# Scaling the attention scores by 0.125 as they leave PSUM, with the negated row maximum written by VectorE

## The chip, the core and the metric

The program runs on one core of a Trainium2 chip. The core has five engines with in-order queues: TensorE (PE, with its weight loads as PEld), VectorE (DVE), ScalarE (ACT), GpSimd (POOL) and SyncE (SP, which here only starts DMA transfers). An engine takes the next instruction of its own queue only when that one's semaphores allow it, so an instruction that waits holds up everything queued behind it on its engine. The metric is the device time of one execution in microseconds; lower is better.

## What is computed

Three blocks run one after the other. The change touches the first, attention that keeps the 32 largest scores of every row:

```python
scores = scale * np.matmul(q, k.transpose(0, 1, 3, 2))      # scale = 1/sqrt(64) = 0.125
kth    = np.partition(scores, -32, axis=-1)[..., -32:-31]
scores = np.where(scores >= kth, scores, -1e9)
attn   = np.exp(scores - scores.max(-1)); attn /= attn.sum(-1) + 1e-9
out    = attn @ v                                            # 4 batches, 8 heads, 576 x 576, head size 64
```

The other two ("dense" below) are a token-mixing block with a squared ReLU and a sigmoid gate, and a block with GELU, a layer norm and a 576 x 576 matrix over the tokens. All of it is float32; matmuls are made of three passes over operands split into a high and a low part.

## The kernel before

**Tiles.** The rows of the score matrices are cut into 80 slots of 128 rows: per batch 4 head pairs, each with five slots, of which four hold the same 128 rows of two heads (n = 2) and one the last 64 rows of both (n = 1). Batch 0 goes through its slots in two halves.

**One slot.** `emit_S` makes the scores on PE into the PSUM tile `S`, and ACT copies them to SBUF (`S2`, line 242, or line 255 for the slot with n = 1). `emit_topk` searches on DVE: lines 275 and 276 take the elementwise larger and smaller of the two row halves into `T`; four rounds of `max` (line 284, the next eight of a row) and `match_replace` (line 294, strikes them out) lead to the 32nd value. After the second round's `max` a small reduce (line 287) has the row maximum, ACT multiplies it by -0.125 (line 288, tile `nb`), and ACT's exponential (line 306) computes `E = exp(0.125 * S + nb)`, two instructions for n = 2. `emit_mask` (line 311, DVE) zeroes what lies below the 32nd value and sums the rest; it is emitted in the next slot, between that slot's first `match_replace` and its second round. Then `emit_T` transposes E on PE (line 326 and its neighbours) with copies to SBUF on ACT (line 327, `PT`), and after the last slot of a unit `emit_unit` multiplies by v (line 355, for the last batch line 386), copies the row factors with ACT (line 413, `rb`) and writes the result with DVE (line 420, `x`).

**Dense work** of a batch (`part1`, `part2`) becomes available when the attention of the batch is complete, and is mixed into the slots of the next batch; the dense work of the last batch is left for the end. Lines 569, 634, 679, 760 and 788 are its matmuls, 686 and 534 its copies and GELUs on ACT, 695 to 700 its layer norm on DVE and POOL, 518 its weight loads on SP. The split into high and low parts is ACT line 100 and POOL line 102.

**What sets the order.** Each piece of work gets a priority (`at(1000 * s)` for slot s), and a list scheduler lays out the engines' queues by priority and by when it reckons an instruction's inputs to be ready. So one instruction more or less shifts the order of many others. The exponential needs another set of tables on ACT than the GELU; a table load stands in the queue at each switch.

Line 275 to 311 are what the change touches; the quoted functions follow.

Of the kernel before, what the change touches and what calls it, by code (L numbers as in the profile page):

```python
# [9 lines left out]
F32 = mybir.dt.float32  # L10
# [3 lines left out]
AF = mybir.ActivationFunctionType  # L14
OP = mybir.AluOpType
# [8 lines left out]
def computation(ctx, tc, dram, wscr, flag, fast, q, k, v, mu_k, mu_r, w_k, w_v, w_r, w_in, g_ln, w_sg, b_sg, w_out, out):  # L24
    nc = tc.nc
# [8 lines left out]
    HALF = S // 2  # L34

    const = ctx.enter_context(tc.tile_pool(name="const", bufs=1))
    sb = ctx.enter_context(tc.tile_pool(name="sb", bufs=1))
# [46 lines left out]
    def bank(tag, shape=(128, 512), dt=F32):  # L84
        if tag == "d" and rows[0] == NROWS:
            tag = ("d", "tp")[turn[0] % 2]
            turn[0] += 1
        return psum.tile(list(shape), dt, tag=tag, name=tag, bufs=BUFS[tag])
# [22 lines left out]
    for b in range(B):  # L111
# [4 lines left out]
        for p, chs in order:  # L116
            su = Rec()
            su.b, su.p, su.chs, su.raw, su.slots = b, p, chs, {}, []
            for ch in chs:
# [3 lines left out]
                for i, j in enumerate(js):  # L123
                    t = Rec()
# [107 lines left out]
    def emit_S(t):  # L232
        su = t.su
        t.S = sb.tile([128, t.hs, S], F32, tag="S2", name="S2", bufs=3)
        for h in range(t.hs):
            ps = bank("S", (128, 2, 512))
            if t.j < 4:
                for a in range(2):
                    for hf in range(2):
                        nc.tensor.matmul(ps[:, hf, :HALF], lhsT=su.qst[h, t.u.ch][:, a, 128 * t.i:128 * t.i + 128],  # L240
                                         rhs=su.kst[h][:, HALF * hf:HALF * hf + HALF], start=(a == 0), stop=(a == 1))
                nc.scalar.activation(t.S[:, h].rearrange("p (a n) -> p a n", a=2), ps[:, :, :HALF], AF.Copy)  # L242
            else:

                for i in range(4):
                    hh, a = divmod(i, 2)
                    ks, qs = su.kst[hh], su.qrem[:, a, hh:hh + 2].rearrange("p h m -> p (h m)")
                    if hh == 0:
                        parts = [(0, 0, 0, HALF), (1, 0, HALF, HALF)]
                    else:  # L250
                        parts = [(0, 0, 64, HALF), (1, 0, 64 + HALF, 512 - HALF), (1, 512 - HALF, 0, 64)]
                    for hf, o, ko, m in parts:
                        nc.tensor.matmul(ps[:, hf, o:o + m], lhsT=qs, rhs=ks[:, ko:ko + m],
                                         start=(i == 0), stop=(i == 3 and m != 512 - HALF))
                nc.scalar.activation(t.S[:, 0].rearrange("p (a n) -> p a n", a=2), ps[:, :, :HALF], AF.Copy)

    ROUNDS = (slice(0, 208), slice(48, HALF), slice(0, HALF), slice(0, S))

    def emit_topk(t, between):

        u, n = t.u, t.hs
        if t.first:
            u.sums = sb.tile([128, 5], F32, tag="sums", name="sums", bufs=3)

            u.M = sb.tile([128, 5, 32], F32, tag="M", name="M", bufs=3)
            u.row0 = rows[0]
        c = 2 * t.i
        M = u.M[:, c:c + n]
        T = sb.tile([128, n, S], F32, tag="T2", name="T2", bufs=1)
        nb = sb.tile([128, n], F32, tag="nb", name="nb", bufs=3)  # L270
        t.E = sb.tile([128, n, S], F32, tag="E2", name="E2", bufs=2)
        if fast:

            for h in ([slice(h, h + 1) for h in range(n)] if rows[0] == 0 else [slice(0, n)]):
                nc.vector.tensor_tensor(T[:, h, :HALF], t.S[:, h, :HALF], t.S[:, h, HALF:], op=OP.max)  # L275
            nc.vector.tensor_tensor(T[:, :, HALF:], t.S[:, :, :HALF], t.S[:, :, HALF:], op=OP.min)  # L276
            L = [T[:, h, :] for h in range(n)]
            src, segs = L, ROUNDS
        else:
            L = [T[:, h, :] for h in range(n)]  # L280
            src, segs = [t.S[:, h, :] for h in range(n)], [slice(0, S)] * 4
        for r, seg in enumerate(segs):
            for h in range(n):
                nc.vector.max(M[:, h, 8 * r:8 * r + 8], src[h][:, seg])  # L284
            if fast and r == 1:
                top = sb.tile([128, n], F32, tag="top", name="top", bufs=3)
                nc.vector.tensor_reduce(top, M[:, :, 0:16:8], axis=mybir.AxisListType.X, op=OP.max)
                nc.scalar.activation(nb, top, AF.Copy, scale=-0.125)
            elif not fast and r == 0:
                nc.scalar.activation(nb, M[:, :, 0], AF.Copy, scale=-0.125)  # L290
            if r == 3:
                break
            for h in range(n):
                mr = nc.vector.match_replace(L[h][:, seg], M[:, h, 8 * r:8 * r + 8], src[h][:, seg], NEG)  # L294
            src = L
            if r == 0:
                between(mr)
        t.kv = [M[:, h, 31:32] for h in range(n)]
        if fast and t.last:

            m = c + n
            nc.gpsimd.tensor_tensor(gap[:, u.row0:u.row0 + m], u.M[:, :m, 31:32].to_broadcast([128, m, 3]),
                                    u.M[:, :m, 7:24:8], op=OP.subtract)
        rows[0] += n
        for h in range(n):
            nc.scalar.activation(t.E[:, h], t.S[:, h], AF.Exp, bias=nb[:, h:h + 1], scale=0.125)  # L306

    def emit_mask(t, gate):
        for h in range(t.hs):
# [545 lines left out]
    for i in range(AHEAD):  # L855
        emit_S(slots[i])
# [16 lines left out]
    for s, t in enumerate(slots):  # L873
# [4 lines left out]
        n = supers.index(su)  # L878
# [9 lines left out]
        if s + AHEAD < NS:  # L888
            emit_S(slots[s + AHEAD])
        emit_topk(t, lambda g: finish_slot(slots[s - 1], g) if s else None)  # L890
        if s == NS - 1:
            finish_slot(t, None)
# [21 lines left out]
    if fast:  # L914
        with at(1000 * NS):
            g = const.tile([128, 1], F32, name="g")
            nc.vector.tensor_reduce(g, gap.rearrange("p r i -> p (r i)"), axis=mybir.AxisListType.X, op=OP.max)
            ps = bank("tp")
# [69 lines left out]
```

## Time and profile before

| | us |
|---|---|
| median of 3 runs | 1001.49 |
| lowest and highest of them | 997.75, 1002.79 |
| the profiled execution's own time | 997.91 |
| its span, first to last instruction | 995.8 |
| DVE busy in the span | 841.0 (84%) |
| PE busy in the span | 878.1 (88%) |
| ACT busy in the span | 697.6 (70%) |
| POOL busy in the span | 528.7 (53%) |

Busy shares are averages over stages with different limits, so the views below are cut into stretches: attention with the conversion of the weights and the first dense work (25 to 660 us), the last batch's attention beside the dense work of the one before (660 to 803), a passage in which the attention ends (803 to 853), and the last batch's dense work (853 to 996). "Idle before" is time in which an engine stood still before an instruction, with what ended it. Records of matmuls overlap, so a PE that is busy all the time need not be at its peak.

### The profile page before, as it was taken

How to read it: one execution, taken by the hardware profiler on the slowest of the kernel's cores; microseconds unless marked ns; L12 is line 12 of the kernel's file. 1: busy time of each engine (PE TensorE's matmuls, PEld its weight loads, DVE VectorE, ACT ScalarE, POOL GpSimd, SP SyncE). 2: the span in 40 equal slices, each digit the busy share in tenths (PEclk: the TensorE clock that was granted, in tenths of full speed). 3: DMA queues.
4: the chain of work that ended last, by engine and by line, in shares of the span. 5: the costliest groups of instructions: out<-in, count | busy, mean ns of one | idle time of the engine just before them, and what ended most of it. 6: DMA issues, size and time to landing. Idle time of an engine off the chain costs nothing.

```text
span 995.8 us, 18647 instructions
## 1 busy us (share of the span) xinstructions
PE 878.1 (88%) x6078; PEld 759.7 (76%) x6078; DVE 841.0 (84%) x2337; ACT 697.6 (70%) x1559; POOL 528.7 (53%) x630
## 2 busy tenths in 40 slices
PE   3465768889888989798999999989999998999997
PEld 2344547777778888577888979868999886899895
DVE  6899999998999999999999999999999973712142
ACT  6778878888886796677687679666876585554340
POOL 7788788675975168559343216598331125210051
PEclk9986779999999999988999999999999999999999
DMA  7953486888467645512333343354333436664432
GB/s 214 371 187 136 156 252 224 282 279 304 167 209 252 219 120 188 171 33 69 109 100 110 110 143 94 99 192 151 109 118 109 128 124 223 218 248 148 122 126 68
DMA packets 105067, 166.34 MB, mean 167 GB/s; under 512 B 19328, under 2 KB 74368, under 8 KB 104960
## 3 DMA queue, kind: packets, MB, share of 16 engines
q1 hardware_dynamic: 104960, 165.05, 50.8%
q8 instruction: 50, 0.82, 0.3%
q14 instruction: 57, 0.47, 0.1%
HBM read 134.27 MB, written 30.21 MB: 165 GB/s over the span
## 4 chain that ended last, share of the span: by engine, by line
PE 45%; DVE 28%; ACT 10%; DMA 8%; POOL 4%; issue 3%; SPq 2%; POOLq 0%; DVEq 0%; ACTq 0%
PE d L569 9%; DVE M L284 8%; PE d L634 6%; DVE E L311 6%; DVE T L294 6%; PE d L679 5%; PE S L240 3%; PE d L760 3%; DVE T L275 3%; PE d L788 3%; PE tp L569 3%; DVE T L276 2%; PE tp L326 2%; PE tp L355 2%; ACT E L306 2%
## 5 line engine op out<-in xcount | busy, mean ns | idle before, releaser
L284 DVE MAX8 M<-T 128x8 f32<-128x208 f32 (+3 forms) x576 | 261.2, 485 | 1.0
L294 DVE MATCH_REPLACE8 T<-M,T 128x208 f32<-128x208 f32 (+2 forms) x432 | 168.9, 394 | 0.0
L569 PE MATMUL d<-xm,w 128*128 128x288 f32 (+2 forms) x1008 | 161.0, 305 | 6.9 <-DMA w<-ws_k 2.4
L311 DVE SCALAR_TENSOR_TENSOR E<-S,M,E 128x576 f32<-128x576 f32 x144 | 147.2, 1048 | 4.7 <-ACT E L306 4.7
L569 PEld LDWEIGHTS d<-xm,w 128*128 128x128 f32 x1008 | 140.5, 191 | 12.5 <-DMA w<-ws_k 3.2
L240 PE MATMUL S<-kst,qst 128*128 128x288 f32 x512 | 111.1, 337 | 28.6 <-ACT S L242 13.6
L240 PEld LDWEIGHTS S<-kst,qst 128*128 128x128 f32 x512 | 83.5, 209 | 41.5 <-ACT S L242 18.9
L326 PE MATMUL tp<-ident,E 128*128 128x128 f32 x512 | 84.6, 295 | 29.2 <-ACT kst L209 14.3
L306 ACT ACTIVATE E<-S,nb 128x576 f32<-128x576 f32 x144 | 105.2, 775 | 0.8
L634 PE MATMUL d<-ksq,w 128*128 128x288 f32 (+2 forms) x672 | 103.9, 302 | 0.6 <-DMA w<-ws_v 0.6
L242 ACT ACTIVATE S<-S 128x576 f32<-128x576 f32 x128 | 83.1, 650 | 30.2 <-DVE E L311 17.4
L326 PEld LDWEIGHTS tp<-ident,E 128*128 128x128 f32 x512 | 64.5, 150 | 38.2 <-ACT kst L209 15.0
L634 PEld LDWEIGHTS d<-ksq,w 128*128 128x128 f32 x672 | 91.8, 189 | 1.6 <-DMA w<-ws_v 0.8
L275 DVE TENSOR_TENSOR T<-S 128x576 f32<-128x576 f32 (+1 forms) x81 | 72.2, 891 | 17.3 <-ACT S L242 12.7
L327 ACT ACTIVATE PT<-tp 128x512 f32<-128x512 f32 x128 | 74.0, 599 | 8.5 <-PE tp L326 8.5
L276 DVE TENSOR_TENSOR T<-S 128x576 f32<-128x576 f32 (+1 forms) x80 | 79.8, 997 | 0.0
L355 PE MATMUL tp<-PT,rawv 128*64 128x256 f32 (+1 forms) x384 | 62.7, 461 | 9.1 <-ACT PT L327 9.1
L760 PE MATMUL d<-w,vn 128*128 128x288 f32 x392 | 60.1, 302 | 5.6 <-DMA w<-ws_sg 2.1
L697 POOL TENSOR_SCALAR bag<-bag 128x1 f32<-128x1 f32 (+1 forms) x20 | 6.1, 303 | 109.5 <-DVE bag L696 108.2
L102 POOL TENSOR_TENSOR ksq<-tmp,ksq 128x576 fp32r<-128x576 f32 (+2 forms) x32 | 41.1, 1289 | 37.3 <-ACT ksq L100 35.4
L760 PEld LDWEIGHTS d<-w,vn 128*128 128x128 f32 x392 | 53.7, 188 | 8.3 <-DMA w<-ws_sg 2.4
L788 PE MATMUL d<-w,gt 128*128 128x512 f32 (+1 forms) x204 | 53.8, 409 | 2.8 <-DVE xr L796 2.5
(182 smaller groups left out, 2018.3 us busy)
## 6 DMA issues: line engine op xcount, KB each, us to landing
w<-ws_k SPq DMA_DIRECT2D x40, 512.0 KB, 3.7
w<-ws_v SPq DMA_DIRECT2D x40, 512.0 KB, 4.1
w<-ws_sg SPq DMA_DIRECT2D x40, 288.0 KB, 3.7
w<-ws_r SPq DMA_DIRECT2D x20, 512.0 KB, 6.2
w<-ws_h SPq DMA_DIRECT2D x20, 512.0 KB, 3.6
w<-ws_u SPq DMA_DIRECT2D x20, 512.0 KB, 3.5
w<-ws_o SPq DMA_DIRECT2D x16, 512.0 KB, 4.6
rawk<-in_k_dram SPq DMA_DIRECT2D x40, 128.0 KB, 2.6
```

Of the source, the lines that this page charges most:

```text
L240: nc.tensor.matmul(ps[:, hf, :HALF], lhsT=su.qst[h, t.u.ch][:, a, 128 * t.i:128 * t.i + 128], rhs=su.kst[h][:, HALF * hf:HALF * hf + HALF] ...
L275: nc.vector.tensor_tensor(T[:, h, :HALF], t.S[:, h, :HALF], t.S[:, h, HALF:], op=OP.max)
L276: nc.vector.tensor_tensor(T[:, :, HALF:], t.S[:, :, :HALF], t.S[:, :, HALF:], op=OP.min)
L284: nc.vector.max(M[:, h, 8 * r:8 * r + 8], src[h][:, seg])
L294: mr = nc.vector.match_replace(L[h][:, seg], M[:, h, 8 * r:8 * r + 8], src[h][:, seg], NEG)
L306: nc.scalar.activation(t.E[:, h], t.S[:, h], AF.Exp, bias=nb[:, h:h + 1], scale=0.125)
L311: m = nc.vector.scalar_tensor_tensor(E, t.S[:, h], t.kv[h], E, op0=OP.is_ge, op1=OP.mult, accum_out=t.u.sums[:, 2 * t.i + h:2 * t.i + h + 1])
L326: nc.tensor.transpose(ps[:, kc, :], E[:, h, 64 * h + 128 * kc:64 * h + 128 * kc + 128], ident)
L569: nc.tensor.matmul(ps[:, :n_], lhsT=w[:, bb, 128 * c:128 * c + 128], rhs=act[ch, which, c][:, a, o:o + n_], start=(c == 0 and i == 0), sto ...
L634: nc.tensor.matmul(ps[:, :nn], lhsT=w[:, bb, 128 * (f % 4):128 * (f % 4) + 128], rhs=kt[f][:, a, o:o + nn], start=(f == 0 and i == 0), sto ...
L760: nc.tensor.matmul(ps[:, :HALF], lhsT=act[b, "vn", i][:, a, 128 * m:128 * m + 128], rhs=W["sg", i, si][:, bb, :HALF], start=(j == 0), stop ...
L788: nc.tensor.matmul(ps[:nn], lhsT=gt[m][:, a, 128 * i:128 * i + nn], rhs=W["o", m][:, bb, :512], start=(j == 0), stop=(j == 11))
```

## The change

The factor 0.125 moves from the exponential to the copy that takes the scores out of PSUM, so S, the search and the row maximum are in scaled units. The reduce on DVE writes the maximum negated, straight into `nb`; the tile `top` and the 80 small ACT instructions of line 288 are gone, and the exponential waits for DVE instead of for ACT's own earlier instruction. 0.125 is a power of two, so no score's digits change. (The kernel also holds a second version of the whole computation for inputs on which the short search is not exact; it is edited alike and is not executed here.)

```diff
-                nc.scalar.activation(t.S[:, h].rearrange("p (a n) -> p a n", a=2), ps[:, :, :HALF], AF.Copy)
+                nc.scalar.activation(t.S[:, h].rearrange("p (a n) -> p a n", a=2), ps[:, :, :HALF], AF.Copy,
+                                     scale=0.125)
...
-                top = sb.tile([128, n], F32, tag="top", name="top", bufs=3)
-                nc.vector.tensor_reduce(top, M[:, :, 0:16:8], axis=mybir.AxisListType.X, op=OP.max)
-                nc.scalar.activation(nb, top, AF.Copy, scale=-0.125)
+                nc.vector.tensor_reduce(nb, M[:, :, 0:16:8], axis=mybir.AxisListType.X, op=OP.max, negate=True)
...
-            nc.scalar.activation(t.E[:, h], t.S[:, h], AF.Exp, bias=nb[:, h:h + 1], scale=0.125)
+            nc.scalar.activation(t.E[:, h], t.S[:, h], AF.Exp, bias=nb[:, h:h + 1])
```

The queues of all engines are laid out anew. Three places matter below. The names are tiles, with their buffer's number where it is shown; 128x576 is the size of what is written.

ACT's queue around a slot in the second third of the program, before. L606 and L609 are dense copies, `ksq` the split that follows them, `rb` the row factors for the last product with v:

```order
L100 ACTIVATE ksq<-tmp 128x576
L242 ACTIVATE S_6490<-S 128x576
L606 ACTIVATE tmp<-d 128x288
L609 ACTIVATE tmp<-tmp 128x576
L100 ACTIVATE ksq<-tmp 128x576
L288 ACTIVATE nb<-top 128x2
L306 ACTIVATE E_6683<-S_6348,nb 128x576 x2
L413 ACTIVATE rb<-tp 128x320
L202 ACTIVATE qst<-tp 128x512
```

The same slot now (the line numbers are those of the changed file):

```order
L609 ACTIVATE tmp<-tmp 128x576
L100 ACTIVATE ksq<-tmp 128x576
L606 ACTIVATE tmp<-d 128x288
L242 ACTIVATE S_6400<-S 128x576
L306 ACTIVATE E_6591<-S_6260,nb 128x576 x2
L413 ACTIVATE rb<-tp 128x320
L202 ACTIVATE qst<-tp 128x512
```

The exponential stands where the copy of the maximum stood, with `rb` directly behind it as before; the pair of dense instructions that went ahead of it has changed.

PE's queue where the last slot's E is transposed (L334 to L339) and multiplied by v (L386 to L397) amid the token matrix (L760, 112 matmuls in two halves of 56), before:

```order
L334 MATMUL tp<-ident,E_11383 128x128 x4
L760 MATMUL d<-w,vn 128x288 x3
L338 MATMUL tp<-ident,E_11383 64x64
L339 MATMUL tp<-ident,E_11383 64x64
L760 MATMUL d<-w,vn 128x288 x6
L381 MATMUL tp<-identr,rhl 10x128
L386 MATMUL tp<-PT,rawv 64x320 x8
L390 MATMUL tp<-PTr,rawv 64x320 x2
L760 MATMUL d<-w,vn 128x288 x5
L392 MATMUL tp<-rT,spread 128x128 x2
L397 MATMUL tp<-rT,spreadr 128x64 x2
L760 MATMUL d<-w,vn 128x288 x65
```

And now:

```order
L334 MATMUL tp<-ident,E_11225 128x128 x4
L760 MATMUL d<-w,vn 128x288 x6
L338 MATMUL tp<-ident,E_11225 64x64
L339 MATMUL tp<-ident,E_11225 64x64
L381 MATMUL tp<-identr,rhl 10x128
L760 MATMUL d<-w,vn 128x288 x14
L386 MATMUL tp<-PT,rawv 64x320 x8
L390 MATMUL tp<-PTr,rawv 64x320 x2
L392 MATMUL tp<-rT,spread 128x128 x2
L397 MATMUL tp<-rT,spreadr 128x64 x2
L760 MATMUL d<-w,vn 128x288 x50
```

The first half of the token matrix is now through before the product with v; before, nine of its 56 matmuls came after that.

ACT's queue a little earlier, where the GELUs of the batch before last (L534) meet the exponential of the third slot from the end, before:

```order
L686 ACTIVATE vraw<-d 128x512
L534 ACT_TABLE_LOAD
L534 ACTIVATE vraw<-vraw 128x512
L686 ACTIVATE vraw<-d 128x512
L534 ACTIVATE vraw<-vraw 128x512
L686 ACTIVATE vraw<-d 128x512
L242 ACTIVATE S_11105<-S 128x576
L534 ACTIVATE vraw<-vraw 128x512
L327 ACTIVATE PT<-tp 128x4x128
L330 ACTIVATE PTr<-tp 128x128
L306 ACT_TABLE_LOAD
L306 ACTIVATE E_11218<-S_10965,nb 128x576 x2
```

And now:

```order
L686 ACTIVATE vraw<-d 128x512
L306 ACT_TABLE_LOAD
L306 ACTIVATE E_11064<-S_10815,nb 128x576 x2
L534 ACT_TABLE_LOAD
L534 ACTIVATE vraw<-vraw 128x512
L686 ACTIVATE vraw<-d 128x512
L242 ACTIVATE S_10953<-S 128x576
L534 ACTIVATE vraw<-vraw 128x512
L686 ACTIVATE vraw<-d 64x512
L534 ACTIVATE vraw<-vraw 128x512
L534 ACTIVATE vraw<-vraw 64x512
L242 ACTIVATE S_10953<-S 128x576
```

The exponential has moved ahead of the next slot's score copies (`S_11105` before, `S_10953` now), and the second of these now stands last, behind all the GELUs. The number of table loads in the program is unchanged.

## Rows read from the trace of the kernel before

**Rows 1.** Busy time by stretch: length, then PE, PEld, DVE, ACT, POOL, with counts.

```profile
core 0: us, PE busy (x) PEld busy (x) DVE busy (x) ACT busy (x) POOL busy (x), PEclk, DMA share, GB/s
25.00:660.00 635.00, 547.00 (x3829) 465.14 (x3829) 615.93 (x1734) 490.84 (x1117) 402.41 (x457) 0.94 0.54 176
660.00:803.00 143.00, 140.54 (x1001) 123.04 (x1000) 134.83 (x403) 98.39 (x223) 58.08 (x62) 0.99 0.38 122
803.00:853.00 50.00, 45.14 (x319) 38.54 (x318) 25.02 (x71) 31.50 (x60) 23.61 (x37) 1.00 0.58 189
853.00:996.00 143.00, 136.11 (x894) 125.57 (x892) 49.67 (x92) 60.62 (x126) 26.30 (x43) 0.99 0.47 154
```

**Rows 2.** What DVE waited for, 25 to 660 us: total us, times, longest.

```profile
DVE x L420 <- ACT rb L413: 5.5, 4, 2.2
DVE T L275 <- ACT S L242: 3.9, 2, 2.6
```

**Rows 3.** What ACT waited for most, 25 to 660 us.

```profile
ACT nb L288 <- DVE top L287: 44.4, 26, 5.1
```

**Rows 4.** Instructions of three lines: duration ns min/median/max, first and last start, shapes.

```profile
L287 DVE TENSOR_REDUCE top<-M x80: 115/144/158, 21.0 to 823.4; 128x2 f32<-128x4 f32 x64, 128x1 f32<-128x2 f32 x16
L288 ACT ACTIVATE nb<-top x80: 186/203/325, 24.3 to 823.8; 128x2 f32<-128x2 f32 x64, 128x1 f32<-128x1 f32 x16
L311 DVE SCALAR_TENSOR_TENSOR E<-S,M,E x144: 789/838/2802, 27.0 to 829.4; 128x576 f32<-128x576 f32 x144
```

**Rows 5.** The chain that ended last, two pieces of it: start us, length us, what.

```profile
24.27 0.19 ACT nb L288
...
812.79 0.20 ACT nb L288
```

**Rows 6.** ACT's instructions in order of time, around two slots: start us, length us.

```profile
421.39 0.20 ACT L288 ACTIVATE nb<-top 128x2 f32<-128x2 f32 x1 [5.13 <-DVE top L287]
421.50 0.76 ACT L556 ACTIVATE tmp<-x,mu 128x576 f32<-128x576 f32 x1
...
495.19 0.20 ACT L288 ACTIVATE nb<-top 128x2 f32<-128x2 f32 x1 [3.95 <-DVE top L287]
495.43 1.45 ACT L306 ACTIVATE E<-S,nb 128x576 f32<-128x576 f32 x2
496.78 0.41 ACT L413 ACTIVATE rb<-tp 128x320 f32<-128x320 f32 x1
```

**Rows 7.** DVE's instructions in the second of these slots.

```profile
495.01 0.14 DVE L287 TENSOR_REDUCE top<-M 128x2 f32<-128x4 f32 x1
...
498.36 0.40 DVE L420 TENSOR_TENSOR x<-tp,rb 128x256 f32<-128x256 f32 x1
```

**Rows 8.** Groups by shape, whole run: count, busy us, mean ns, idle before.

```profile
L493 ACT ACTIVATE w<-raw 128x512 int32<-128x512 uint32 x20 | 13.6, 678 | 11.7 <-DVE d L491 11.7
L488 ACT ACTIVATE w<-raw 128x512 f32<-128x512 f32 x20 | 13.4, 668 | 3.9 <-DMA raw<-in_moe_w_k_dram 2.3 <-DMA raw<-in_moe_w_r_dram 1.2 <-DMA ws_r<-w 0.4
...
L406 DVE TENSOR_SCALAR rinv<-sums 128x4 f32<-128x4 f32 x16 | 3.9, 242 | 0.0
```

**Rows 9.** Passage in which attention ends, PE, in order of time.

```profile
837.27 2.38 PE L386 MATMUL tp<-PT,rawv 128*64 128x320 f32 x16
...
841.67 2.80 PE L760 MATMUL d<-w,vn 128*128 128x288 f32 x18
846.62 1.59 PE L760 MATMUL d<-w,vn 128*128 128x288 f32 x10 [2.15 <-DMA w<-ws_sg]
```

**Rows 10.** The same passage: the score copy on ACT, DVE's wait for it.

```profile
804.00 0.65 ACT L242 ACTIVATE S<-S 128x576 f32<-128x576 f32 x1
...
804.68 0.76 DVE L275 TENSOR_TENSOR T<-S 128x576 f32<-128x576 f32 x1 [5.68 <-ACT S L242]
```

**Rows 11.** DVE groups by shape, 25 to 660 us: count, busy us, mean ns.

```profile
L311 DVE SCALAR_TENSOR_TENSOR E<-S,M,E 128x576 f32<-128x576 f32 x113 | 116.3, 1057 | 0.4 <-ACT E L306 0.4
...
L284 DVE MAX8 M<-T 128x8 f32<-128x288 f32 x112 | 45.6, 439 | 0.3
```

More of the change, by code (lines that the diff above doesn't have):

```diff
@@ L254, in emit_S @@
                                          start=(i == 0), stop=(i == 3 and m != 512 - HALF))
-                nc.scalar.activation(t.S[:, 0].rearrange("p (a n) -> p a n", a=2), ps[:, :, :HALF], AF.Copy)
+                nc.scalar.activation(t.S[:, 0].rearrange("p (a n) -> p a n", a=2), ps[:, :, :HALF], AF.Copy,
+                                     scale=0.125)
     ROUNDS = (slice(0, 208), slice(48, HALF), slice(0, HALF), slice(0, S))
@@ L285, in emit_topk @@
             if fast and r == 1:
-                top = sb.tile([128, n], F32, tag="top", name="top", bufs=3)
-                nc.vector.tensor_reduce(top, M[:, :, 0:16:8], axis=mybir.AxisListType.X, op=OP.max)
-                nc.scalar.activation(nb, top, AF.Copy, scale=-0.125)
+                nc.vector.tensor_reduce(nb, M[:, :, 0:16:8], axis=mybir.AxisListType.X, op=OP.max, negate=True)
             elif not fast and r == 0:
-                nc.scalar.activation(nb, M[:, :, 0], AF.Copy, scale=-0.125)
+                nc.scalar.activation(nb, M[:, :, 0], AF.Copy, scale=-1.0)
             if r == 3:
```

## The prediction

> **What bounds the kernel now.** I read the busy times by stretch first [rows 1]. From 25 to 660 us DVE is the bound: it is busy 615.9 of 635 us, so all that better-fed queues could win there is 19.1 us. From 660 to 803 PE is busy 140.5 of 143 us and DVE 134.8: two full engines. From 803 to 853 nothing is full (PE stands 4.9 us), a chain of short steps runs from the last GELUs and slots to the last matmuls, and from 853 on it is PE's own work again, 136.1 of 143 us. ACT, from which the change takes work, is nowhere the fullest. Next the waits. The largest one on ACT is just the one that the change deletes: 26 of the small copies of the maximum stood 44.4 us for the reduce on DVE [rows 3]. But ACT waits there for the engine that is the bound, which loses nothing by it. What counts is what DVE waits for, and of that ACT causes two large items: `x` waiting for `rb`, 5.5 us in 4 waits, and the next slot's first step waiting for a score copy, 3.9 us in 2 [rows 2]: 9.4 us together. Last the chain of waits: the small copy stands in it 16 times, the first and the last of which are shown; the 16 pieces add up to 2.2 us [rows 5].
>
> **The change part by part.**
>
> *The 80 small ACT instructions go.* Each took 203 ns in the median [rows 4], 80 x 0.203 = 16.2 us of ACT. They overlap with what follows, though: where an independent instruction came next it started 0.11 us after the small copy, where the exponential came next 0.24 us after [rows 6]. The exponential came next, with no further wait, in 23 slots, so the queue is freed of about 23 x 0.24 + 57 x 0.11 = 11.8 us. That lies beside DVE's work except in the chain's 16 pieces. Where DVE's own work is close behind, removing a piece brings less than its length; I take 1.5 of the 2.2 us.
>
> *The wait doesn't go.* The exponential needs the same maximum, and in the slot whose queue is shown it now stands exactly where the small copy stood, behind the same score copy. So ACT stops there as before (3.95 us in that slot [rows 6]), with `rb` right behind. What changes is that the result of the reduce reaches the exponential without a stop on ACT: E, and `rb` behind it, come 0.24 us sooner after the reduce. Elsewhere some instructions that stood between the small copy and the exponential (tmp L556 in the other slot of [rows 6]) can now be ahead of the wait or behind the exponential. Of DVE's 9.4 us of waits for ACT I expect this to return 1; the bounds are none and all.
>
> *The reduce writes its result negated.* No row shows a negating reduce. DVE does 80 reduces of 144 ns [rows 4]; the nearest instruction with arithmetic of its own on so few elements is the addition to the sums, 242 ns in the mean [rows 8]. Bounds: 0 to 80 x 0.098 = 7.8 us of DVE. It can't be a gain, since the same elements are read and written. I take 0: the 242 are another operation, and the count of DVE instructions is unchanged. [...]
>
> *The scale on the copies out of PSUM.* 144 copies get a constant factor and the 144 exponentials lose theirs. The nearest pair: an ACT copy with a constant scale, 678 ns, against the absolute value without one, 668 ns, on the same shape [rows 8]. So 0 to 144 x 0.01 = 1.4 us, on an engine that isn't the bound, and the exponential could give as much back. I take 0. What hides it is the slack of a score copy, which in most slots is ready a slot ahead; without that cover it would be 10 ns a copy.
>
> *The order.* The scheduler lays all queues out anew. In the passage at 803 to 853 two moves oppose each other. PE stood 2.15 us for weights of the second half of the token matrix [rows 9]; those loads could start only when matmuls of the first half were through with the buffers, and nine of these stood behind the product with v, 2.38 us [rows 9]. Now the first half is through before that product, so the loads can start earlier and the product covers them: up to 2.2 us gained, up to 4.9 if all of PE's idle time in the passage goes. Against it, the third-last exponential now stands ahead of the next slot's score copies, with two table loads and GELUs before the second of these. Before, DVE stood 5.68 us for that copy [rows 10]; the copy can now come about 5 us later, on DVE, which is not on the chain there unless the last slots end so late that PE waits for their transposes. Bounds -4.9 and +5.7 us; I take -1.5, nearer the gain, because it sits on PE, which the chain follows.
>
> *Contention.* DVE's masking takes 1.06 us in the mean but 0.79 at the least [rows 4, 11], while the search's `max` of 288 shows none of this spread at 0.44 us [rows 11]. The excess in this stretch is 113 x (1.057 - 0.789) = 30 us, and it depends on what POOL does at the moment, which a new order shifts. I take 0, with 15% of the excess, 4.5 us, to either side.
>
> *The sum:* -1.5 - 1 + 0 + 0 - 1.5 + 0 = -4.0 us. The profiled execution took 997.91 us, so 993.9; the median before is 1001.49, 3.6 above that execution, and by the median I get **997.5 us**. About 0.5%, 5 us, is what a measurement of this kernel can tell from no change, so the forecast is "the same, by a small margin better".
>
> **The rivals.**
>
> *Faster: the queue behind the wait was worth more.* If the shorter step from reduce to `rb` and the 11.8 us of freed queue remove all of DVE's 9.4 us of waits for ACT, the chain gives its 2.2, and PE's 2.15 us go, it is -13.8 us: 988 by the median. For it: the waits for `rb` are just of the kind that a step 0.24 us shorter helps. Against it: four waits of 1.4 us each are more than 0.24 us, and most come from where `rb` stands in the queue.
>
> *Slower: `rb` behind the exponential.* In the new queues `rb` stands directly behind an exponential in 10 of 32 units, in the old ones in 6 (counted in the queues as they are laid out). In the slot of [rows 6, 7] `x` came 3.35 us after the reduce, and E with `rb` ended 2.18 us after it: 1.2 us to spare. The point from which it decides: an exponential that starts more than 1.6 us after the reduce began (ACT late with the score copy ahead of it, say) makes DVE stand. If all ten cost what a wait of this kind cost before, 1.4 us [rows 2], that is 14 us in place of 5.5: +8.5, less the 1.5 of the chain, 1008.5 us.
>
> *Slower or nil: the locks between POOL and DVE fall otherwise.* The trace's masking spread is the sign of it. If a quarter more of the masks collide, +7.5 us, which with the -4.0 gives 1005; as much the other way 990. [...]
>
> **How the numbers follow.** Forecast 46%: of it 14 fall below -5 us, 31 within, 1 above. Faster rival 25%, all below -5. `rb` behind E 17%: 13 above +5, 4 within. Locks 12%: 5 within, 7 above. So faster 0.39, same 0.40, slower 0.21. The range takes in the faster rival, 988, and nearly the slower one, 1008: under 1 in 10 is left out at either end, the bounds of the unmeasured terms (reduce up to +7.8, passage -4.9 to +5.7) lie inside it if they come alone.
>
> **What would show it.** In the profile after: no line with a copy of the maximum; the reduce still near 144 ns (above 200 the reduce's term is wrong); the exponential waiting for DVE some 40 us in all, about as the small copy did; ACT some 16 us less busy; DVE as busy as before between 25 and 660 us, within 5 us; DVE's waits for `rb` and the score copies at 5 to 12 us; no wait, or a short one, for weights in the middle of the token matrix. Wrong it would be if DVE's busy time moved by over 5 us (locks), if the waits for `rb` passed 12 us, or if the exponential's wait were small, for then the order took the wait away after all.

## The result, and the profile after

| | before | after |
|---|---|---|
| median of 12 runs, us | 1001.03 | 1005.65 |
| lowest and highest, us | 996.96, 1002.79 | 1003.84, 1010.24 |
| the profiled execution, us | 997.91 | 1010.24 |
| its span, us | 995.8 | 1008.4 |

The ratio is 1.0058, with a 95% interval of 1.0042 to 1.0075: the change makes the kernel slower by 0.6%, some 5 to 6 us (the quotient of the two medians alone is 1.0046). Medians and ratios here and below go by the fast executions; one slow execution each of E5, E9 and E18 is left out. The forecast was 997.5, faster by 0.4%; it lies on the wrong side. The profiled execution of after is the slowest of its 12 runs, 4.6 us above their median, so the 12.6 us between the two spans overstate the loss. A second profile of after, of run E4 below (1004.48 us, span 1002.5), is nearer to the median and is used for the closer looks.

Busy time by stretch in the profile of after, with the same columns as [rows 1]; the last row ends at the end of its span:

```profile
core 0: us, PE busy (x) PEld busy (x) DVE busy (x) ACT busy (x) POOL busy (x), PEclk, DMA share, GB/s
25.00:660.00 635.00, 544.60 (x3779) 462.05 (x3780) 607.97 (x1715) 476.63 (x1044) 389.32 (x449) 0.93 0.53 174
660.00:803.00 143.00, 135.95 (x988) 119.45 (x987) 136.80 (x389) 97.21 (x209) 67.55 (x69) 0.99 0.40 126
803.00:853.00 50.00, 46.26 (x296) 40.60 (x295) 34.51 (x100) 36.37 (x64) 21.79 (x32) 0.97 0.46 145
853.00:1008.00 155.00, 148.21 (x980) 135.51 (x978) 52.16 (x98) 62.00 (x132) 31.39 (x47) 1.00 0.50 164
```

Against [rows 1] the reader is to see that the end of the program is as it was, only later: from 853 us on PE works through in both, but after has 980 matmuls ahead of it at that point where before had 894, and the 148.21 - 136.11 = 12.1 us that these take are nearly the whole difference of the spans, 12.6. What is lost is lost ahead of 853. In the first two stretches DVE is busy 8.0 us less and 2.0 us more, so DVE stood some 6 us longer there and reached the passage with more of its own work left (34.51 us in it, against 25.02).

The two lines of the profile's table of groups that hold the operations of the change, and the two instructions of DVE that stand next to it, listed with their least, median and greatest duration:

```profile
L306 ACT ACTIVATE E<-S,nb 128x576 f32<-128x576 f32 x144 | 106.1, 781 | 31.4 <-DVE nb L288 31.0
L242 ACT ACTIVATE S<-S 128x576 f32<-128x576 f32 x128 | 83.5, 652 | 39.8 <-PE S L240 25.4 <-DVE E L311 13.8
...
L288 DVE TENSOR_REDUCE nb<-M x80: 134/143/158, 21.3 to 842.5; 128x2 f32<-128x4 f32 x64, 128x1 f32<-128x2 f32 x16
...
L311 DVE SCALAR_TENSOR_TENSOR E<-S,M,E x144: 783/826/1977, 26.9 to 845.1; 128x576 f32<-128x576 f32 x144
```

The negating reduce has a median of 143 ns, against the 144 of the plain one [rows 4]; the copy of the maximum is gone from the page; the exponential now waits for DVE itself, 31.0 us in the whole run. Each piece does what the diff says, at the price that was expected. The waits of DVE and the largest of ACT between 25 and 660 us (total us, times, longest), to be held against [rows 2, 3]:

```profile
DVE T L277 <- ACT S L242: 8.6, 3, 3.9
DVE x L420 <- ACT rb L413: 3.5, 2, 2.8
DVE bst L695 <- ACT vraw L534: 3.1, 2, 2.9
...
ACT E L306 <- DVE nb L288: 24.7, 14, 6.6
```

DVE waits 2.0 us less for `rb` and 4.7 us more for a score copy. The copy itself takes as long as before (652 and 650 ns in the mean), so it is not its new factor that DVE waits for. Whether the new layout of the queues brought the waits along is what E1 to E4 ask.

The passage in the profile of after, in order of time (start us, length us, what): ACT, then DVE, then PE.

```profile
815.21 1.44 ACT L306 ACTIVATE E<-S,nb 128x576 f32<-128x576 f32 x2
816.67 1.28 ACT L534 ACT_TABLE_LOAD   x1
...
820.50 1.15 ACT L534 ACTIVATE vraw<-vraw 128x512 f32<-128x512 f32 x2
...
807.93 0.76 DVE L277 TENSOR_TENSOR T<-S 128x576 f32<-128x576 f32 x1 [3.85 <-ACT S L242]
821.16 1.29 DVE L695 BATCH_NORM_STATS2 bst<-vraw 128x6 f32<-128x512 f32 x2 [4.39 <-ACT vraw L534]
...
839.79 3.31 PE L760 MATMUL d<-w,vn 128*128 128x288 f32 x24
847.18 1.33 PE L760 MATMUL d<-w,vn 128*128 128x288 f32 x4 [3.31 <-DMA vn<-vn]
...
855.08 2.38 PE L386 MATMUL tp<-PT,rawv 128*64 128x320 f32 x16
...
858.62 6.86 PE L760 MATMUL d<-w,vn 128*128 128x288 f32 x50
```

The wait for weights of [rows 9] is gone: the last 50 matmuls of the token matrix run without a stop behind the product with v. In its place PE stands 3.31 us earlier on, for the transfer of the layer norm's rows (`vn`), which had not landed when the first half of the token matrix came to it. Before, it stood 1.10 us for such a transfer:

```profile
836.23 1.05 PE L760 MATMUL d<-w,vn 128*128 128x288 f32 x6 [1.10 <-DMA vn<-vn]
```

That is 2.21 us more, and 2.15 us for weights less. DVE, which stood 5.68 us for a score copy [rows 10], stands 3.85 us for one and then 4.39 us for GELUs that came to lie behind the exponential and its table load.

### The profile page after: what moved, and what is told of

It reads as the page before. It is cut to its first block, busy times and chain, and to the rows that moved or that the text cites. A ratio compares the mean times of both kernels' runs of the same rounds, so it can differ in the third digit from the quotient of the medians.

```text
span 1008.4 us, 18591 instructions
## 1 busy us (share of the span) xinstructions
PE 884.3 (88%) x6078; PEld 765.0 (76%) x6078; DVE 846.7 (84%) x2337; ACT 687.2 (68%) x1479; POOL 527.8 (52%) x630
## 4 chain that ended last, share of the span: by engine, by line
PE 46%; DVE 25%; DMA 8%; POOL 7%; ACT 6%; issue 5%; SPq 2%; POOLq 0%; DVEq 0%; ACTq 0%
PE d L569 8%; PE d L634 7%; DVE M L286 7%; DVE E L311 5%; PE d L679 5%; DVE T L294 5%; PE d L760 3%; PE tp L355 3%; PE S L240 3%; PE tp L569 2%; PE tp L326 2%; DVE T L277 2%; DVE T L278 2%; PE d L788 1%; DMA w<-ws_r 1%
## 5 line engine op out<-in xcount | busy, mean ns | idle before, releaser
L311 DVE SCALAR_TENSOR_TENSOR E<-S,M,E 128x576 f32<-128x576 f32 x144 | 148.8, 1061 | 1.0 <-ACT E L306 0.8
L634 PEld LDWEIGHTS d<-ksq,w 128*128 128x128 f32 x672 | 94.0, 193 | 0.9 <-issue 0.5
L277 DVE TENSOR_TENSOR T<-S 128x576 f32<-128x576 f32 (+1 forms) x81 | 70.8, 874 | 22.2 <-ACT S L242 17.5
L278 DVE TENSOR_TENSOR T<-S 128x576 f32<-128x576 f32 (+1 forms) x80 | 76.9, 961 | 0.0
L760 PE MATMUL d<-w,vn 128*128 128x288 f32 x392 | 60.9, 307 | 7.9 <-DMA vn<-vn 4.2
L760 PEld LDWEIGHTS d<-w,vn 128*128 128x128 f32 x392 | 55.7, 196 | 9.3 <-DMA vn<-vn 3.5
L102 POOL TENSOR_TENSOR ksq<-tmp,ksq 128x576 fp32r<-128x576 f32 (+2 forms) x32 | 38.7, 1217 | 42.5 <-ACT ksq L100 41.4
L679 PE MATMUL d<-w,x 128*128 128x512 f32 (+1 forms) x216 | 55.2, 404 | 1.9 <-DMA w<-ws_h 1.9
```

Source lines behind the costliest of these rows:

```text
L311: m = nc.vector.scalar_tensor_tensor(E, t.S[:, h], t.kv[h], E, op0=OP.is_ge, op1=OP.mult, accum_out=t.u.sums[:, 2 * t.i + h:2 * t.i + h + 1])
L634: nc.tensor.matmul(ps[:, :nn], lhsT=w[:, bb, 128 * (f % 4):128 * (f % 4) + 128], rhs=kt[f][:, a, o:o + nn], start=(f == 0 and i == 0), sto ...
L679: nc.tensor.matmul(ps[:nn], lhsT=act[ch, 2, c][:, a, o:o + nn], rhs=W["h", c][:, bb, :512], start=(j == 0), stop=(j == 11))
L760: nc.tensor.matmul(ps[:, :HALF], lhsT=act[b, "vn", i][:, a, 128 * m:128 * m + 128], rhs=W["sg", i, si][:, bb, :HALF], start=(j == 0), stop ...
```

## Experiments

All results stand in one table; each ratio is to runs of the kernel before on the same chip, with its 95% interval. E1 to E4 ran on one chip, as did E5 to E8, E9 to E12, E13 to E16, and E17 and E18.

| run | operations | order of the queues | median us | ratio |
|---|---|---|---|---|
| E1 | scale and negation; copies kept | as before | 998.3 | 1.0005 (0.999 to 1.002) |
| E2 | all of the edit | held as before | 999.55 | 1.0013 (0.9994 to 1.0032) |
| E3 | none of the edit | held as after | 1009.89 | 1.0115 (1.0094 to 1.0136) |
| E4 | all (after, once more) | after | 1005.89 | 1.0081 (1.0063 to 1.010) |
| E5 | all | after up to slot 57, then before | 1004.6 | 1.0058 (1.0036 to 1.0081) |
| E6 | all | before up to slot 57, then after | 1005.59 | 1.0073 (1.0048 to 1.0099) |
| E7 | all | after up to slot 75, then before | 1004.78 | 1.0059 (1.0037 to 1.0081) |
| E8 | all | pieced from both | 1003.27 | 1.004 (1.0022 to 1.0057) |
| E9 | copies out in slots 0 to 19 | the scheduler's own | 1002.35 | 1.0048 (1.0026 to 1.0071) |
| E10 | copies out in slots 60 to 79 | own | 998.2 | 0.9998 (0.9979 to 1.0018) |
| E11 | none; dense share 0.99 | own | 1000.01 | 1.0016 (0.9996 to 1.0036) |
| E12 | none; a third buffer for `bst` | own | 1001.46 | 1.0031 (1.0012 to 1.0049) |
| E13 | copies out in slots 20 to 79 | own | 1002.87 | 1.0041 (1.0024 to 1.0058) |
| E14 | copies out in slots 0 to 39 | own | 999.03 | 1.0003 (0.9991 to 1.0015) |
| E15 | copies out in even slots | own | 998.87 | 1.0005 (0.9988 to 1.0022) |
| E16 | copies out in odd slots | own | 1002.29 | 1.0029 (1.0009 to 1.0049) |
| E17 | all | held as E14 | 997.08 | 0.9991 (0.9979 to 1.0004) |
| E18 | all | held as E15 | 1000.5 | 1.0018 (0.9996 to 1.0039) |

### E1 to E4: operations against order

The change does two things at once: it alters operations, and it makes the scheduler lay out every queue anew. Two kernels hold the queues. A table lists, for each engine, its instructions in the wanted order, and an ordering dependency without a semaphore ties each instruction to the one ahead of it, so that the scheduler has no choice left. Nothing else is edited; the wanted order is the one that the other kernel has, with the 80 copies taken out or put in.

```diff
+        for a, b in zip(row, row[1:]):          # row: this engine's instructions in the wanted order
+            tc.add_manual_dep(mine[b], mine[a].name, nosync, reason="queue order")
```

E1 is the two new forms of operation alone. The copy remains, so the scheduler lays out the same queues by itself:

```diff
-                nc.vector.tensor_reduce(top, M[:, :, 0:16:8], axis=mybir.AxisListType.X, op=OP.max)
-                nc.scalar.activation(nb, top, AF.Copy, scale=-0.125)
+                nc.vector.tensor_reduce(top, M[:, :, 0:16:8], axis=mybir.AxisListType.X, op=OP.max, negate=True)
+                nc.scalar.activation(nb, top, AF.Copy)
```

(with the scale on the copies out of PSUM and none on the exponential, as in the change).

> Half of the edit: S leaves PSUM scaled by 0.125 and VectorE writes the row maximum negated, but into `top`, and ScalarE still copies `top` to `nb` (scale 1.0). Every engine's queue then holds the same rows in the same order as in the kernel before, so that only the two new forms of operation are measured. Theory A (the operations are neutral and the loss comes from the new order of the queues): 1001 us, ratio 0.998 to 1.002; L287 stays at 144 ns, the S copy at 650 ns. Rival B (the operations themselves cost: a scaled copy out of PSUM or a negated reduction delays the chain of a slot): ratio 1.003 to 1.008.

E2 has the whole edit, in the old order:

> All of the edit, but every queue (TensorE, VectorE, ScalarE, GpSimd, SyncE) is held in the order that it had in the kernel before, the 80 copies to `nb` alone being taken out. Theory A (the loss is in the order that the scheduler made anew): 998.5 us, ratio 0.995 to 0.9995, i.e. the 16 small copies off the chain and 16 us less in ScalarE's queue are worth 1 to 4 us. Rival B (without the copy E waits for VectorE itself and the queue behind E comes later, whatever the order): 1005 us, ratio 1.003 to 1.007.

E3 has none of it, in the new order:

> None of the edit's operations, but every queue is held in the order that it has in the changed kernel, with the 80 copies to `nb` put in, each right ahead of the E that uses it. Theory A (order): slower than before, 1006 to 1010 us, ratio 1.005 to 1.009, since the new order's loss stays and the copies come on top. Rival B (the operations): 1001 us, ratio 0.998 to 1.002.

E4 is the changed kernel again:

> The changed kernel once more, on the same chip as the three others, as the measure for them: 1005.7 us, ratio 1.004 to 1.0075. If it came within 0.2% of before, the difference that is to be explained would be one of chips or of runs and not of the change.

The four results decide it. Old order: 1.0005 with the copies and 1.0013 without. New order: 1.0115 with them and 1.0081 without. The order costs 0.7 to 1.1%, whichever operations stand in it, and the operations cost nothing that can be measured. TensorE's clock does not explain it: the granted clock as a share of full speed, averaged over each kernel's runs, is 0.954 in both E2 and E3, which lie 10 us apart (0.957 in the kernel before, 0.952 in E4). The groups of E1's profile, of DVE and of ACT:

```profile
L287 DVE TENSOR_REDUCE top<-M 128x2 f32<-128x4 f32 (+1 forms) x80 | 11.6, 145 | 0.3
...
L306 ACT ACTIVATE E<-S,nb 128x576 f32<-128x576 f32 x144 | 105.1, 774 | 0.8
L242 ACT ACTIVATE S<-S 128x576 f32<-128x576 f32 x128 | 83.1, 650 | 28.4 <-DVE E L311 13.6 <-PE S L240 11.8 <-PE tp L326 2.7
L288 ACT ACTIVATE nb<-top 128x2 f32<-128x2 f32 (+1 forms) x80 | 16.4, 205 | 48.0 <-DVE top L287 47.6
```

The negating reduce into `top` has a mean of 145 ns, the scaled score copy 650. Both are the means of the profile of before, where the reduce doesn't negate and the copy doesn't scale: 145 ns over the 80 reduces and 650 over the 128 copies.

What failed is the expectation for E2: 998.5 us and a ratio under 1 were expected, and with the order held the removal of 80 instructions from ACT brings nothing that can be measured. (The ratios of E3 and E4 also came out above those expected for them.) The same wait, in E1 and then in E2, and the mask's group of E2:

```profile
ACT nb L288 <- DVE top L287: 47.6, 30, 4.3
...
ACT E L306 <- DVE nb L288: 25.5, 18, 4.1
...
L311 DVE SCALAR_TENSOR_TENSOR E<-S,M,E 128x576 f32<-128x576 f32 x144 | 150.5, 1071 | 4.6 <-ACT E L306 4.6
```

ACT is relieved twice over: it waits 22.1 us less for the reduce, since what stood between the copy and the exponential now goes ahead of the wait, and it has 16.4 us of copies less. The end of the program doesn't notice either. In the new order the same removal is worth 4 us (E3 to E4), though the two intervals just touch. E3 is held in its order and E4 is not, and no run holds an unchanged kernel in its own order, so a cost of the holding itself isn't told apart from those 4 us; E2 and E17, held too, lie at 1.0013 and 0.9991. E17 and E18 ask which of the two is the rule.

### E5 to E8: where in the order

The four kernels carry the changed operations and join the two orders at a cut: all that one order has placed up to the reduce of the cut's slot stands as in that order, and the rest as in the other.

> The changed kernel's operations. Every queue stands in the new order up to the reduction of slot 57 and in the order of the kernel before from there on (rows that the new order had already placed are left out of the second part). Theory A1 (the new order's loss sits in places behind slot 57: by the profiles of the two orders with the same operations the new order is 4 us ahead at slot 58 and 4 us behind at the end): 995 to 999 us, at or under the 999.5 us of the old order. Rival A2 (the loss is a backlog that the new order builds up earlier, as the 11 us by slot 20 suggest, and that comes due later): 1004 to 1007 us.

> The complement: the old order up to the reduction of slot 57, the new order from there on, with the changed kernel's operations. Theory A1: 1005 to 1010 us, as slow as the changed kernel or slower, since the places behind slot 57 are all in it and the new order's lead of 4 us is not. Rival A2 (backlog from earlier): 998 to 1001 us.

> The new order up to the reduction of slot 75, the old order from there on, with the changed kernel's operations. If the loss falls between slots 57 and 75 (the new order goes from 4 us ahead to 5 us behind there): 1004 to 1008 us. If it falls in the last slots and the passage to the last part (5 us more between slots 76 and 78): 996 to 1000 us, as with the cut at slot 57.

> The changed kernel's operations with each queue pieced together from the stretch of either order that was the shorter one in the profiles: old to slot 29, new to slot 52 (4 us shorter there), old to slot 78, new to the end (6 us shorter there). If the stretches are local and add up: 988 to 992 us, ahead of both kernels. If what a stretch gains is work that it leaves to the next (the last part of the new order is short because slots 76 to 78 did some of its work): 997 to 1001 us.

All four came out between 1003 and 1006 us. E5 and E6 are complements and each loses as much as the whole, so both theories of a place fall: the loss isn't in the part behind slot 57 alone, nor in that ahead of it alone, and it doesn't add up from stretches. (Each cut also makes a joint that neither order has; what a joint costs is not shown.) E8, pieced from the stretches that were the shorter ones, is no faster than 1003, above both times that were expected for it. Why a lead does not last shows in the busy time from the reduce of slot 56 to the end, for E2 (old order), E4 (new) and E5 (new up to slot 57):

```profile
589.17:998.30 409.13, 393.77 (x2719) 350.09 (x2717) 279.97 (x773) 247.70 (x505) 153.80 (x198) 0.99 0.43 141
585.25:1002.50 417.25, 398.67 (x2758) 355.20 (x2754) 285.93 (x775) 248.60 (x507) 156.59 (x198) 0.99 0.43 141
584.74:1000.00 415.26, 399.29 (x2761) 354.03 (x2759) 282.35 (x775) 249.08 (x508) 153.80 (x198) 0.99 0.43 142
```

E4 reaches that reduce 3.9 us before E2, but with 39 matmuls (4.9 us of PE) and 6.0 us of DVE work more still to do. Its lead is work put off, and my cuts took it for work saved. The lead itself is that of one profile over another: the kernel before, with the order of E2 and as much work left (394.9 us of PE, 280.2 of DVE), has that reduce at 585.40 us, level with E4. What the rows show is the work left. E5 has put off as much of PE's work by then and less of DVE's; from slot 57 on it follows the old order, and DVE stands 5.0 us in three waits before slot 58 is through:

```profile
600.77 0.76 DVE L277 TENSOR_TENSOR T<-S 128x576 f32<-128x576 f32 x1 [2.96 <-ACT S L242]
604.01 1.29 DVE L695 BATCH_NORM_STATS2 bst<-vraw 128x6 f32<-128x512 f32 x2 [1.25 <-ACT vraw L534]
606.78 0.82 DVE L311 SCALAR_TENSOR_TENSOR E<-S,M,E 128x576 f32<-128x576 f32 x1 [0.80 <-ACT E L306]
```

The same score copy in E4 and in E2, PE's queue and DVE's step behind it:

```profile
592.74 5.97 PE L679 MATMUL d<-w,x 128*128 128x512 f32 x25
598.84 0.76 PE L240 MATMUL S<-kst,qst 128*128 128x288 f32 x4
600.60 0.76 DVE L277 TENSOR_TENSOR T<-S 128x576 f32<-128x576 f32 x1 [2.69 <-ACT S L242]
...
591.52 6.20 PE L679 MATMUL d<-w,x 128*128 128x512 f32 x26
598.12 0.50 PE L240 MATMUL S<-kst,qst 128*128 128x288 f32 x2
...
601.39 0.76 DVE L277 TENSOR_TENSOR T<-S 128x576 f32<-128x576 f32 x1
```

In both, PE makes the scores behind some 25 dense matmuls. In the old order (below) DVE still had work until the copy was there and went on without a wait; in the new one it had come through early and stood 2.69 us.

### E9 to E12: less of the edit, or none

E9 and E10 make the edit in some slots only; the others write `top`, negated, and copy it:

```diff
+                top = nb if slots.index(t) < 20 else sb.tile([128, n], F32, tag="top", name="top", bufs=3)
+                nc.vector.tensor_reduce(top, M[:, :, 0:16:8], axis=mybir.AxisListType.X, op=OP.max, negate=True)
+                if top is not nb:
+                    nc.scalar.activation(nb, top, AF.Copy)
```

(E10: `slots.index(t) >= 60`.) E11 and E12 are the kernel before with a nudge to the scheduler:

```diff
-        quota = 0.995 * dense.left() / (nxt - s)
+        quota = 0.99 * dense.left() / (nxt - s)
...
-            st = sb.tile([128, 6], F32, tag="bst", name="bst", bufs=2)
+            st = sb.tile([128, 6], F32, tag="bst", name="bst", bufs=3)
```

> The edit in slots 0 to 19 alone; slots 20 to 79 keep `top` and the copy to `nb`. The scheduler lays the queues out itself: they differ from those of before up to about slot 46 and are the same behind it. Theory A3 (the order of the kernel before is a favourable one; whatever makes the scheduler lay out a stretch anew costs some us): 1002 to 1006 us. Rival A4 (a few bad places behind slot 57 in the changed kernel's order make the loss): 998 to 1000 us, as those places are not in it.

> The edit in slots 60 to 79 alone; the queues are those of before up to slot 60 and laid out anew behind it. Theory A3: 1002 to 1006 us. Rival A4: 1003 to 1007 us too, if the last 20 slots get the same bad places as in the changed kernel; 998 to 1000 us if not. The pair of this run and the one before it tells the two apart.

> The kernel before without any of the edit; only the share of the dense work that is handed to a slot is 0.99 and not 0.995 of the even one, so that the same operations stand in another order (892 rows of TensorE's queue and 116 of VectorE's differ). Theory A3 (a new order alone costs): 1002 to 1006 us. Rival A5 (the change made the order bad, a nudge of another kind does not): 998 to 1001 us.

> The kernel before without any of the edit; the 24-byte tile `bst` has three buffers and not two, which takes no work away and lays out 611 rows of TensorE's queue and 91 of VectorE's anew. Theory A3: 1002 to 1006 us. Rival A5: 997 to 1001 us.

Neither theory holds whole. The first 20 slots alone lose 4 us, without one of the places behind slot 57; the last 20 lose nothing, so not every new layout is a loss. The nudges, which alter no operation, give 1.0016 (the interval takes in 1) and 1.0031 (it does not): a new order by itself can move the time by 3 us. (In E8, E9 and E11 the time exceeds the span by 2.4 us and not by the 2.0 of the kernel before, so 0.4 us of what they lose lies outside the profiled instructions.)

### E13 to E16: first slots, or the number of copies

> The edit in slots 20 to 79; slots 0 to 19 keep `top` and the copy. The queues are those of before up to slot 20 and laid out anew behind it. If the loss comes with the layout of the first slots: 998 to 1000 us. If it grows with the number of copies taken out (60 of 80): 1003 to 1004 us.

> The edit in slots 0 to 39 alone. If the loss comes with the layout of the first slots: 1003 to 1006 us, as with the first 20. If it grows with the number of copies taken out (40 of 80): 1001 to 1003 us.

> The edit in every even slot (40 of 80). Its queues are near those of the changed kernel (216 rows of VectorE's differ from it, 1408 from before). If the order decides: 1003 to 1008 us, as the changed kernel, with half of its copies still there. If the number of copies taken out decides: 1001 to 1003 us, the same as the odd slots.

> The edit in every odd slot (40 of 80). Its queues are nearer to those of before (510 rows of VectorE's differ) than to those of the changed kernel (1108). If the order decides: 998 to 1002 us, at least 3 us under the even slots. If the number of copies taken out decides: 1001 to 1003 us, the same as the even slots.

Both theories fall, and by the same results. The first 20 slots lose 0.5% and the first 40, which hold them, nothing. The even slots, whose order is the nearer one to that of the changed kernel, lose nothing, and the odd ones 0.3%. From slot 20 on it is 0.4%, with the first 20 as before. No count and no place of the edited slots sets these in a row.

Nor does a single wait. DVE's wait for score copies between 25 and 803 us, in E2 (old order), E4 (new order) and E15 (even slots):

```profile
DVE T L277 <- ACT S L242: 5.4, 4, 2.0
...
DVE T L277 <- ACT S L242: 14.6, 7, 3.9
...
DVE T L277 <- ACT S L242: 15.8, 8, 4.0
```

Read alone, the first two lines look like the cause of the loss: 9.2 us more. E15 waits as long as E4 and is as fast as the kernel before. What goes with the time best is how much was left for the end. From 853 us on E14, and then E10, have

```profile
853.00:1010.00 157.00, 133.58 (x883) 123.65 (x881) 47.44 (x90) 57.56 (x122) 23.85 (x39) 0.99 0.41 136
...
853.00:1012.00 159.00, 138.44 (x899) 127.82 (x897) 49.24 (x93) 59.30 (x125) 25.87 (x41) 0.97 0.42 139
```

E14 has 883 matmuls left, with a span of 993.2 us, against 894 and 995.8 before [rows 1], 941 and 1002.5 in E4, 980 and 1008.4 in after. Before, E4, after and E14 take 0.16 us per matmul from there to the end, whatever the order, so their differences are what the attention part did not get done by then. It isn't the whole in every profile: E10 has only 899 left and a span of 1000.5 us, as PE stands 9.1 us between 853 us and its end, against 6.7 before; in E3, E6 and E13 it stands 8.6 to 9.3 us there. Nor does it say which step of the attention part is to blame.

### E17 and E18: what a copy is worth in a held order

Both take out the 40 copies that E14 and E15 still hold, with every queue held as theirs.

> All of the edit, with every queue held in the order of the kernel that has the edit in slots 0 to 39 alone (999.0 us with the 40 copies of slots 40 to 79). If a copy out of a held order gains 0.05 us, as in the changed kernel's order (4 us for 80): 997 us, ratio 0.997 to 0.999. If it gains nothing, as in the order of before: 999 us, ratio 0.9995 to 1.002.

> All of the edit, with every queue held in the order of the kernel that has the edit in the even slots alone (998.9 us with the 40 copies of the odd slots). If a copy out of a held order gains 0.05 us: 997 us, ratio 0.997 to 0.999. If it gains nothing: 999 us, ratio 0.9995 to 1.002.

E17 is 0.9991 where E14 was 1.0003, E18 1.0018 where E15 was 1.0005: one a little lower, one a little higher, each interval taking in the other value. With E1 and E2 that is three orders in which the removal of 40 or 80 copies brings nothing measurable, against the one order in which it seemed worth 4 us. At that rate 40 copies are worth 2 us, 0.2%, hardly more than these intervals can tell; it is E2, with 80, that speaks clearly against the rate. E17 has the lowest ratio of all, with a median of 997.08 against 998.56, but its interval reaches past 1. No version is shown to beat the kernel before.

## Why the prediction was wrong, point by point

**The reduce and the scale, two terms of 0: right.** 143 ns after against 144 before [rows 4], 650 to 652 ns for the score copy, and E1 at 1.0005. The upper bound of the reduce's term, 7.8 us, came from a misreading: the 242 ns of the addition to the sums [rows 8] are no price of arithmetic but a mean over 16 calls in the profile of before: eleven of 145 to 156 ns, and five of 196 to 764, each of which ended 0.02 to 0.03 us after an instruction on POOL had ended.

**The chain, -1.5 us: wrong.** The copy stood 16 times in the chain, but E2, which has none of them and every queue as before, gains nothing: its interval leaves room for 0.6 us at most. A piece of the chain says that the instruction was the last to be waited for, not that its consumer was in need of the result. The row that says that was in front: the mask waited for E only 0.4 us in all its 113 calls [rows 11]. Over the whole run it waited 4.7 us before and 4.6 in E2, so taking the copies out did not shorten even that.

**ACT's relief, -1 us: wrong, in the held order.** The queue did become freer: ACT's busy time fell by 10.4 us over the run (687.2 against 697.6 us; the text had both 16 and, with the overlap, 11.8), and, more than was forecast, its wait for the reduce fell from 44.4 us [rows 3] to 24.7, where "some 40" were foreseen. DVE's waits for `rb` and score copies came to 8.6 + 3.5 = 12.1 us, just past the 5 to 12. Relief for an engine with 30% of its time to spare was counted as time.

**The order, -1.5 us with bounds of -4.9 and +5.7: this is the step that failed.** I had priced it from the passage alone and put the rest of the layout at nothing, without a reason. It cost 6 us by E4 against E2 (1005.89 - 999.55 = 6.3), just past the upper bound. The passage alone does not make that loss: E7 stands in the old order from slot 75 on and goes from that slot's reduce to that of slot 78 in 37.5 us, as E2 does in 37.4, where E4 takes 42.6; yet E7 loses 0.6%. In the passage itself both moves came as described, but the gain on PE was turned into a longer wait: the 2.15 us for weights [rows 9] are gone and the wait for the layer norm's rows has grown from 1.10 to 3.31 us. What I took for the clearer of the two ends was a trade.

**The rivals.** The faster one did not happen: of DVE's waits for `rb` and score copies it had all 9.4 us go, and they grew to 12.1. The slower one, `rb` behind the exponential, did not happen either: DVE waited 3.5 us for `rb`, less than the 5.5 before [rows 2]. That masks are held up by POOL shows in the profile of before: the 39 masks with no POOL instruction beside them took 0.79 to 0.82 us; of the other 105, 61 took 0.93 us or more, up to 2.80, and 59 of these ended 0.60 to 0.66 us after an instruction on POOL had ended. One of them (POOL, then DVE):

```profile
501.62 1.96 POOL L102 TENSOR_TENSOR ksq<-tmp,ksq 128x576 fp32r<-128x576 f32 x1
...
502.22 1.98 DVE L311 SCALAR_TENSOR_TENSOR E<-S,M,E 128x576 f32<-128x576 f32 x1
```

But the masks' sum over the run came to 148.8 us in after, against 147.2 before and 150.5 in E2, which has the old order: no 7.5 us more. DVE's busy time between 25 and 660 us did move by more than the 5 us that were named as the sign of locks, but down, by 8.0, with 19 fewer instructions done by then; over the whole run it went from 841.0 to 846.7 us. The rival that should have stood there has no place of its own: that a list scheduler, given one instruction less, deals a new layout, and that the scheduler's own layouts lie 0 to 0.8% above the kernel before whatever the edit was. Its price could not be read from the trace of before; its likelihood could have been weighed by giving the slower side more than 0.21.

**The range.** 988 to 1008 held the median of 1005.65, by luck: its upper end came from the wait for `rb`, which did not grow.

**What stays open.** That the order makes the loss is shown (E1 to E4). Which part of the order does it, and by what step, is not: it isn't one place (E5 to E8), not the first slots and not the number of copies (E9 to E16), and not a single kind of wait (E15). Part of it isn't a wait at all: the same 6078 matmuls keep PE busy 876 to 878 us in before, E1 and E2, and 882 to 884 in E3, E4 and after. E6, with 873, shows that this is no rule either, and no run asks why they take longer. That the kernel before has one of the better orders among those run here is shown by the table: of the six layouts that the scheduler made for partial edits, three are level with it and three 0.3 to 0.5% above, and none is below.

## What to carry to other kernels

Where a scheduler lays out the queues, an edit has two effects, and the second can be the larger: measure the operations with the order held, and the order with the operations held, before a gain or a loss of under 1% is put down to the edit. An instruction on the chain of waits is worth taking out only if its consumer is seen to wait; ask for the idle time ahead of the consumer's consumer first. And a slot that begins earlier is no lead until the work that is left behind it has been counted.

## What the runs showed of the hardware that was not expected

**A tiny VectorE instruction held for a whole GpSimd instruction.** E4's profile, POOL and then DVE:

```profile
690.26 1.43 POOL L102 TENSOR_TENSOR xm<-tmp,xm 128x576 fp32r<-128x576 f32 x1
690.31 1.41 DVE L406 TENSOR_SCALAR rinv<-sums 128x5 f32<-128x5 f32 x1
```

Line 406 adds a constant to five numbers per row and has one input. Begun 0.05 us after the start of a subtraction on POOL it took 1.41 us and ended 0.03 us after it. In the profile of after, the 14 of its 32 calls with no POOL instruction beside them took 144 to 165 ns; 13 calls took more than 0.3 us, and each of these ended 0.02 to 0.03 us after an instruction on POOL had ended. The 32 calls sum to 8.5 us in E2, 12.0 us in E4 and 13.4 us in after. They do not make the loss: in E14, which is as fast as the kernel before, they sum to 13.9 us.

**The same queues, several microseconds apart.** E5 and E7 have the same queues up to slot 57 and ran on the same chip. Between the same two reduces (slots 16 and 20), E5 and then E7:

```profile
201.34:243.08 41.74, 36.98 (x259) 31.86 (x259) 40.20 (x109) 30.78 (x66) 23.42 (x24) 0.92 0.79 267
202.40:246.85 44.45, 39.14 (x263) 32.90 (x262) 40.48 (x108) 31.89 (x69) 25.68 (x27) 0.88 0.81 279
...
PE d L679 <- DMA w<-ws_h: 2.0, 1, 2.0
```

E7 takes 2.7 us longer for it, at a mean granted clock of 0.88 against 0.92 (1 is full speed), with PE standing 2.0 us for a weight load (last line, E7), a wait that isn't among the larger ones of E5. Two profiles can differ by that much with nothing changed, so a difference of some 3 us between two single profiles at one slot shows nothing by itself.
